# Stages 12 and 13 scaled and transposed earlier, and one second product moved ahead of the last state visit, in a fused RWKV and MLP kernel

## The chip, the cores and the metric

The kernel runs on one core of one Trainium2 chip. The metric is the device time of one execution in microseconds (us).

## The reference

A linear attention over 4 batches, 8 heads, 768 tokens and 48 channels is followed by a two-layer MLP on 3072 tokens of 384 channels:

```python
for t in range(S):
    cur = einsum('bhd,bhe->bhde', u * k[t], v[t])
    y[t] = einsum('bhd,bhde->bhe', r[t], state + cur)
    state = w * state + einsum('bhd,bhe->bhde', k[t], v[t])
x = y.transpose(0, 2, 1, 3).reshape(B * S, H * D)
h = x @ w_in                       # 384 -> 2048
out = maximum(0.01 * h, h) @ w_out # 2048 -> 384
```

## The kernel before

The tokens are cut into chunks of 128, which makes 24 stages: four batches by six chunks, the four batches side by side. Stages n and n+4 are neighbours in time of one batch, and the state goes from one to the other. Within a chunk the recurrence is a masked product of matrices. From stage 12 on an even stage is "swapped": its two halves of 64 tokens lie in exchanged order, and one load (L266) brings one half for two stages, so that stage 12 needs the loads named 12 and 14.

The order of all work is written out by hand in the string ORDER. Each word is one step, and `run` walks through the words and puts the step's instructions at the end of the queue of their engine. Every engine works through its queue in that order; semaphores are set where one engine needs another's result. PSUM banks are given out in the order of the words too. The words that matter here, for a stage n:

- `k`, `r`, `v`: the loads of the stage, issued from POOL (GpSimd).
- `Pq`, `Pk` (prep_half, L437, DVE): r and k scaled by tables of decays into qk. `X..T` (turn_dma, L442): a DMA transpose of qk into tp, issued from SP.
- `q` (row_sums, L466, L468, L470, DVE): three operations that give s_tok, the sums for the token's own term. `Q` (diag_tile, L477, POOL): two tiles with s_tok on the diagonal, written into at.
- `A` or `B` (L529, L548, PE): the products of transposed r and k, for one stage or a pair; `Ma`, `Mb` (L563, DVE) copy their lower triangle into at. B6 is the pair 12 and 13, B7 is 14 and 15, B11 is 22 and 23.
- `Y` (L719, PE): y from at, v, tp and the state; `y` (L733, ACT) copies it to xT.
- `K` (L595, PE): the stage's part of the state; `S` (L671, DVE) adds it to the state; `s` (L689, DVE) multiplies by the decay over a chunk.
- `J` (L758, PE): the MLP's first product for two stages in eight tiles, `j` (L769, ACT) their leaky ReLU into gT.
- `H` (L782, PE): the MLP's second product for one stage; `h` (L794, ACT) copies it to out_sb, and SP issues the store (L802, or L799 for swapped stages).

A round in the middle of the kernel takes two stages through each step: two Y, two K, one B, eight J and two H.

SP's queue holds both transposes and stores, in the order of the words. POOL's holds the loads and the diagonal tiles. There are six buffers each of qk, tp, at and of the state, four each of s_tok, ku, rku, sum_t and out_sb, and two of xT and gT.

Of the kernel before, what the change touches and what calls it, by code (L numbers as in the profile page):

```python
# [35 lines left out]
j2.1 P6k P7k G2.0 r7 q7 X6T J2.6 j2.6 J2.3 j2.3 k8 G3.0 J2.7 j2.7 k9 r9 j2.2 J2.5 P7q g3.0 g2.3 X7T J2.0 H1 h1 r8 q8  # L36
g2.0 Q6 P9k j2.0 P8k H0 j2.5 H3 Q7 A6 P9q X9T P8q X8T v6 A7 M6a v7 M7a g2.1 ts qtabs ktabs H2 h2 v9 v11 v10 M6b Y6 M7b
tris y6 Q8 Y7 y7 K5 r11 K6 S6 r10 k10 S5 v8 k11 k12 k14 K7 S7 q9 Q9 h0 h3 J3.0 j3.0 J3.1 j3.1 J3.2 j3.2 J3.3 j3.3 J3.4
j3.4 J3.5 j3.5 J3.6 j3.6 J3.7 j3.7 A8 A9 M8a M8b M9a M9b P10q P10k X10T P11q P11k X11T r12 r14 k13 r13 q10 Q10 q11 Q11
H4 h4 Y8 Y9 y8 y9 K8 K9 S8 S9 s8 s9 H5 h5 J4.0 j4.0 J4.1 j4.1 J4.2 j4.2 J4.3 j4.3 J4.4 j4.4 J4.5 j4.5 J4.6 j4.6 J4.7  # L40
j4.7 P12q P12k X12T P13q P13k X13T q12 q13 A10 A11 M10a M10b M11a M11b v12 v14 k15 r15 v13 v15 Q12 Q13 H6 h6 H7 h7 Y10
Y11 y10 y11 K10 K11 B6 M12a M12b M13a M13b S10 S11 P14q P14k X14T P15q P15k X15T s10 s11 q14 q15 J5.0 j5.0 J5.1 j5.1
k16 k18 r16 r18 k17 r17 Q14 Q15 J5.2 j5.2 J5.3 j5.3 J5.4 j5.4 J5.5 j5.5 J5.6 j5.6 J5.7 j5.7 H8 h8 H9 h9 Y12 Y13 y12
y13 K12 K13 B7 M14a M14b M15a M15b S12 S13 P16q P16k X16T P17q P17k X17T s12 s13 q16 q17 J6.0 j6.0 J6.1 j6.1 v16 v18
k19 r19 v17 v19 Q16 Q17 J6.2 j6.2 J6.3 j6.3 J6.4 j6.4 J6.5 j6.5 J6.6 j6.6 J6.7 j6.7 H10 h10 H11 h11 Y14 Y15 y14 y15
K14 K15 B8 M16a M16b M17a M17b S14 S15 P18q P18k X18T P19q P19k X19T s14 s15 q18 q19 J7.0 j7.0 J7.1 j7.1 k20 k22 r20
r22 k21 r21 Q18 Q19 J7.2 j7.2 J7.3 j7.3 J7.4 j7.4 J7.5 j7.5 J7.6 j7.6 J7.7 j7.7 H12 h12 H13 h13 Y16 Y17 y16 y17 K16
K17 B9 M18a M18b M19a M19b S16 S17 P20q P20k X20T P21q P21k X21T s16 s17 q20 q21 J8.0 j8.0 J8.1 j8.1 v20 v22 k23 r23
v21 v23 Q20 Q21 J8.2 j8.2 J8.3 j8.3 J8.4 j8.4 J8.5 j8.5 J8.6 j8.6 J8.7 j8.7 H14 h14 H15 h15 Y18 Y19 y18 y19 K18 K19
B10 M20a M20b M21a M21b S18 S19 P22q P22k X22T P23q P23k X23T s18 s19 q22 q23 J9.0 j9.0 J9.1 j9.1 Q22 Q23 J9.2 j9.2  # L50
J9.3 j9.3 J9.4 j9.4 J9.5 j9.5 J9.6 j9.6 J9.7 j9.7 H16 h16 Y20 Y21 y20 y21 B11 M22a M22b M23a M23b H17 h17 J10.0 j10.0
J10.1 j10.1 J10.2 j10.2 J10.3 j10.3 J10.4 j10.4 J10.5 j10.5 J10.6 j10.6 J10.7 j10.7 H18 h18 Y22 Y23 y22 y23 H19 h19
J11.0 j11.0 J11.1 j11.1 J11.2 j11.2 J11.3 j11.3 J11.4 j11.4 J11.5 j11.5 J11.6 j11.6 J11.7 j11.7 H20 h20 H21 h21 H22
h22
"""


# [855 lines left out]
```

## Time and profile before

| | us |
|---|---|
| median of 3 runs | 168.83 (167.63 to 169.45) |
| the profiled execution's own time | 167.48 |
| its span, first to last instruction | 165.6 |
| PE busy | 159.2 (96%) |
| DVE busy | 106.6 (64%) |
| ACT busy | 90.2 (54%) |
| POOL busy | 109.5 (66%) |

The granted clock of TensorE is 1.00 throughout. PE is the matmul unit, PEld its weight loads, DVE the vector engine, ACT the scalar engine, POOL GpSimd and SP the engine that only issues. Times in the profile are counted from the span's start. A row of a timeline gives start, length, engine, line, operation and tiles; in brackets stands the idle time before it and what ended that.

### The profile page before, as it was taken

The numbers are of one execution on the slowest core, as the hardware profiler recorded it, in microseconds if no ns is written. First come the engines' busy times: TensorE is split into PE (matmuls) and PEld (weight loads), VectorE is DVE, ScalarE is ACT, GpSimd is POOL, SyncE is SP. The second block draws the span as 40 slices with busy tenths as digits, with TensorE's granted clock in tenths as the row PEclk, the third lists the DMA queues.
The fourth block names the chain that finished last, engine by engine and source line by source line (L and its number), as shares of the span: only waits on it lengthen the run. The fifth ranks groups of instructions, "written<-read, shape, count | busy, mean of one in ns | idle before, by whom it ended". The sixth has DMA issues, their size and how long they took to land.

```text
span 165.6 us, 5519 instructions
## 1 busy us (share of the span) xinstructions
PE 159.2 (96%) x2397; PEld 122.3 (74%) x2397; DVE 106.6 (64%) x254; ACT 90.2 (54%) x170; POOL 109.5 (66%) x125
## 2 busy tenths in 40 slices
PE   4899999999999999999999999999999999999993
PEld 4678999986568678668668678678678668678663
DVE  7789998278777699948939939939939970000000
ACT  3855893875078339346447437438439429449121
POOL 8999798987999969999099399299370360000000
DMA  7999999999999998999969969969950621020023
GB/s 107 149 143 158 172 189 187 182 151 175 91 175 211 123 127 176 131 180 138 92 153 105 141 150 82 130 170 82 157 131 7 127 51 48 0 64 35 16 82 99
DMA packets 101366, 20.23 MB, mean 122 GB/s; under 512 B 94555, under 2 KB 101342, under 8 KB 101342
## 3 DMA queue, kind: packets, MB, share of 16 engines
q0 software_dynamic: 76512, 10.03, 92.8%
q1 hardware_dynamic: 23790, 9.65, 29.1%
q8 instruction: 19, 0.31, 0.8%
q10 hardware_dynamic: 1040, 0.20, 0.6%
q14 instruction: 5, 0.04, 0.1%
HBM read 20.45 MB, written 4.72 MB: 152 GB/s over the span
## 4 chain that ended last, share of the span: by engine, by line
PE 91%; DMA 4%; POOL 2%; ACT 1%; issue 1%; POOLq 0%; ACTq 0%
PE ps L758 39%; PE ps L782 38%; PE ps L719 6%; DMA v_sb<-in_v_dram 4%; PE ps L529 2%; PE ps L548 2%; PE ps L500 1%; PE ps L604 1%; POOL k_sb L269 1%; PE ps L595 1%; POOL r_sb L269 1%; PE ps L712 1%; ACT out_sb L794 0%; POOL w_in_sb L279 0%; ACT xT L733 0%
## 5 line engine op out<-in xcount | busy, mean ns | idle before, releaser
L758 PE MATMUL ps<-xT,w_in_sb 128*128 128x256 bf16 (+1 forms) x672 | 66.5, 259 | 0.0
L782 PE MATMUL ps<-w_out_sb,gT 128*128 128x384 bf16 (+2 forms) x400 | 64.8, 320 | 0.0
L769 ACT ACTIVATE gT<-ps 128x512 bf16<-128x512 f32 x96 | 56.3, 598 | 14.1 <-PE ps L758 10.1
L758 PEld LDWEIGHTS ps<-xT,w_in_sb 128*128 128x128 bf16 x672 | 57.7, 98 | 6.3
L477 POOL TENSOR_TENSOR at<-ident,s_tok 128x512 bf16<-128x512 bf16 x40 | 42.1, 1082 | 25.1 <-DVE s_tok L470 25.1
L782 PEld LDWEIGHTS ps<-w_out_sb,gT 128*128 128x128 bf16 x400 | 38.0, 98 | 23.0
L794 ACT ACTIVATE out_sb<-ps 128x384 f32<-128x384 f32 (+2 forms) x25 | 11.8, 478 | 46.4 <-PE ps L782 46.4
L563 DVE CAST_PREDICATED at<-mask,ps 128x512 bf16<-128x512 uint16 x28 | 17.9, 685 | 3.2 <-PE ps L529 3.0
L563 DVE CAST_PREDICATED at<-mask_s,ps 128x512 bf16<-128x512 uint16 x12 | 7.7, 687 | 14.2 <-PE ps L548 13.8
L269 POOL DMA_DIRECT2D v_sb<-in_v_dram x18 | 16.4, 927 | 0.0
L269 POOL DMA_DIRECT2D r_sb<-in_r_dram x17 | 15.7, 930 | 0.1
L269 POOL DMA_DIRECT2D k_sb<-in_k_dram x17 | 15.7, 927 | 0.0
L468 DVE TENSOR_TENSOR rku<-r_sb,ku 128x384 bf16<-128x384 bf16 x20 | 12.2, 612 | 1.4 <-DMA r_sb<-in_r_dram 0.7
L733 ACT ACTIVATE xT<-ps 128x384 bf16<-128x384 f32 x24 | 10.8, 490 | 3.1 <-PE ps L719 3.0
L470 DVE TENSOR_REDUCE s_tok<-rku 128x8 f32<-128x384 bf16 x20 | 11.1, 553 | 0.7
L719 PE MATMUL ps<-at,v_sb 128*32 128x128 bf16 x384 | 10.8, 223 | 0.0
L719 PEld LDWEIGHTS ps<-tp,st 128*32 128x32 bf16 x240 | 7.3, 96 | 3.0 <-issue 2.9
L466 DVE TENSOR_TENSOR ku<-k_sb,u_tab 128x384 bf16<-128x384 bf16 x20 | 7.9, 394 | 2.0 <-DMA k_sb<-in_k_dram 1.8
L719 PEld LDWEIGHTS ps<-at,v_sb 128*32 128x32 bf16 x384 | 8.8, 98 | 0.5 <-issue 0.2
L719 PE MATMUL ps<-tp,st 128*32 128x128 bf16 x240 | 9.1, 221 | 0.0
L671 DVE TENSOR_TENSOR sum_t<-ps,st 64x192 bf16<-64x192 f32 x24 | 8.5, 353 | 0.6
L437 DVE TENSOR_TENSOR qk<-k_sb,ktab 128x384 bf16<-128x384 bf16 x17 | 7.5, 447 | 1.0 <-DMA k_sb<-in_k_dram 1.0
(82 smaller groups left out, 124.1 us busy)
## 6 DMA issues: line engine op xcount, KB each, us to landing
out_dram<-out_sb SPq DMA_DIRECT2D x17, 192.0 KB, 3.3
v_sb<-in_v_dram POOLq DMA_DIRECT2D x24, 96.0 KB, 4.6
r_sb<-in_r_dram POOLq DMA_DIRECT2D x23, 96.0 KB, 4.9
k_sb<-in_k_dram POOLq DMA_DIRECT2D x23, 96.0 KB, 5.6
w_in_sb<-in_moe_w_in_dram POOLq DMA_DIRECT2D x4, 384.0 KB, 6.4
w_out_sb<-in_moe_w_out_dram POOLq DMA_DIRECT2D x4, 384.0 KB, 7.0
out_dram<-out_sb SPq DMA_DIRECT2D x12, 96.0 KB, 2.2
tp<-qk SPq DMA_TRANSPOSE x18, 4.4
```

The costliest lines, as they stand in the source:

```text
L269: add("pool", lambda: G.dma_start(dst, src), R=pace, W=[(which, n)], dma=f"{which}{n}")
L468: add("dve", lambda: V.tensor_tensor(rku[i2][:, :], r_of(n), ku[i2][:, :], ALU.mult), R=loaded("r", n) + [("ku", i2)], W=[("rku", i2)])
L470: add("dve", lambda: V.tensor_reduce(s_tok[i2][:, :], hd(rku[i2][:, :]), AX.X, ALU.add), R=[("rku", i2)], W=[("s", i2)])
L477: add("pool", lambda hh=hh, s_of=s_of: G.tensor_tensor(at[ia][:, hh, :, :], ident[:, :].unsqueeze(1).to_broadcast([128, NP, 128]), s_of.un ...
L563: add("dve", lambda: V.copy_predicated(at[n % NAT][:, hh, :, :], tri[:, :].bitcast(mybir.dt.uint16).unsqueeze(1).to_broadcast([128, NP, 12 ...
L671: add("dve", lambda part=part: V.tensor_tensor(both[part], kv[part[0]], st[n % NT][part], ALU.add), R=[key, ("st", n % NT)], W=[("sum", n ...
L719: last = PE.matmul(ps_y[32 * q:32 * q + 32, 128 * s:128 * s + 128], a, m, start=not whole and step == 0, stop=step == len(columns[q]) - 1)
L733: add("act", lambda: A.activation(xT[ix][:, :, 128 * slot:128 * slot + 128], ps_y[:, 0:HD].rearrange("p (s t) -> p s t", t=128), AF.Copy), ...
L758: last = PE.matmul(ps_g[:, step * f:step * f + step], w_in_sb[:, s, 128 * fb:128 * fb + 128], xT[ix][:, s, t], start=s == 0, stop=s == NSL ...
L769: add("act", lambda: A.activation(gT[ig][:, fb0:fb0 + count, t], ps_g[:, :].rearrange("p (f t) -> p f t", t=128 * width), AF.Prelu, alpha= ...
L782: last = PE.matmul(ps_o[:, 0:c1 - c0], gT[ig][:, s, 128 * slot:128 * slot + 128], w_out_sb[:, s, c0:c1], start=s == 0, stop=s == NFB - 1)
L794: add("act", lambda: A.activation(out_sb[io][:, c0:c1], ps_o[:, 0:c1 - c0], AF.Copy), R=[key], W=held)
```

## The change

Only ORDER changes. Word by word, with the line breaks of the string taken out:

```diff
 r12 r14 k13 r13 q10 Q10
-q11 Q11
+P12q P12k X12T
 H4 h4 Y8 Y9 y8 y9 K8 K9 S8 S9
+q11 Q11 P13q P13k X13T
 s8 s9 H5 h5 J4.0 j4.0
...
 J4.7 j4.7
-P12q P12k X12T P13q P13k X13T
 q12 q13 A10 A11 M10a M10b M11a M11b
...
 H16 h16
+H17 h17
 Y20 Y21 y20 y21 B11 M22a M22b M23a M23b
-H17 h17
 J10.0 j10.0
```

On DVE, the scaling of stage 12 now stands right behind the sums of stage 10, then S8 and S9, then the sums of stage 11, the scaling of 13, and s8 and s9. POOL's own order is the same as before, and so is PE's but for H17, which goes ahead of Y20 and Y21; on ACT h17 goes ahead of y20 and y21. On SP the transpose of stage 12 goes ahead of the store of stage 4, and that of stage 13 ahead of the store of stage 5. Some PSUM banks are other ones at the end: before, the eight tiles of J10 took the banks left by h16, y20, y21, the four masks of 22 and 23, and h17, in this order; now the first takes that of h16, the second that of h17, the third and fourth those of y20 and y21, and the last four those of the masks.

More of the change, by code (lines that the diff above doesn't have):

```diff
@@ L38 @@
 tris y6 Q8 Y7 y7 K5 r11 K6 S6 r10 k10 S5 v8 k11 k12 k14 K7 S7 q9 Q9 h0 h3 J3.0 j3.0 J3.1 j3.1 J3.2 j3.2 J3.3 j3.3 J3.4
[L39 to L52, printed above, removed]
@@ L53 @@
-J11.0 j11.0 J11.1 j11.1 J11.2 j11.2 J11.3 j11.3 J11.4 j11.4 J11.5 j11.5 J11.6 j11.6 J11.7 j11.7 H20 h20 H21 h21 H22
-h22
+j3.4 J3.5 j3.5 J3.6 j3.6 J3.7 j3.7 A8 A9 M8a M8b M9a M9b P10q P10k X10T P11q P11k X11T r12 r14 k13 r13 q10 Q10 P12q
+P12k X12T H4 h4 Y8 Y9 y8 y9 K8 K9 S8 S9 q11 Q11 P13q P13k X13T s8 s9 H5 h5 J4.0 j4.0 J4.1 j4.1 J4.2 j4.2 J4.3 j4.3
+J4.4 j4.4 J4.5 j4.5 J4.6 j4.6 J4.7 j4.7 q12 q13 A10 A11 M10a M10b M11a M11b v12 v14 k15 r15 v13 v15 Q12 Q13 H6 h6 H7
+h7 Y10 Y11 y10 y11 K10 K11 B6 M12a M12b M13a M13b S10 S11 P14q P14k X14T P15q P15k X15T s10 s11 q14 q15 J5.0 j5.0 J5.1
@@ new lines @@
+j5.1 k16 k18 r16 r18 k17 r17 Q14 Q15 J5.2 j5.2 J5.3 j5.3 J5.4 j5.4 J5.5 j5.5 J5.6 j5.6 J5.7 j5.7 H8 h8 H9 h9 Y12 Y13
+y12 y13 K12 K13 B7 M14a M14b M15a M15b S12 S13 P16q P16k X16T P17q P17k X17T s12 s13 q16 q17 J6.0 j6.0 J6.1 j6.1 v16
+v18 k19 r19 v17 v19 Q16 Q17 J6.2 j6.2 J6.3 j6.3 J6.4 j6.4 J6.5 j6.5 J6.6 j6.6 J6.7 j6.7 H10 h10 H11 h11 Y14 Y15 y14
+y15 K14 K15 B8 M16a M16b M17a M17b S14 S15 P18q P18k X18T P19q P19k X19T s14 s15 q18 q19 J7.0 j7.0 J7.1 j7.1 k20 k22
+r20 r22 k21 r21 Q18 Q19 J7.2 j7.2 J7.3 j7.3 J7.4 j7.4 J7.5 j7.5 J7.6 j7.6 J7.7 j7.7 H12 h12 H13 h13 Y16 Y17 y16 y17
@@ new lines @@
+K16 K17 B9 M18a M18b M19a M19b S16 S17 P20q P20k X20T P21q P21k X21T s16 s17 q20 q21 J8.0 j8.0 J8.1 j8.1 v20 v22 k23
+r23 v21 v23 Q20 Q21 J8.2 j8.2 J8.3 j8.3 J8.4 j8.4 J8.5 j8.5 J8.6 j8.6 J8.7 j8.7 H14 h14 H15 h15 Y18 Y19 y18 y19 K18
+K19 B10 M20a M20b M21a M21b S18 S19 P22q P22k X22T P23q P23k X23T s18 s19 q22 q23 J9.0 j9.0 J9.1 j9.1 Q22 Q23 J9.2
+j9.2 J9.3 j9.3 J9.4 j9.4 J9.5 j9.5 J9.6 j9.6 J9.7 j9.7 H16 h16 H17 h17 Y20 Y21 y20 y21 B11 M22a M22b M23a M23b J10.0
+j10.0 J10.1 j10.1 J10.2 j10.2 J10.3 j10.3 J10.4 j10.4 J10.5 j10.5 J10.6 j10.6 J10.7 j10.7 H18 h18 Y22 Y23 y22 y23 H19
@@ L55 @@
+h19 J11.0 j11.0 J11.1 j11.1 J11.2 j11.2 J11.3 j11.3 J11.4 j11.4 J11.5 j11.5 J11.6 j11.6 J11.7 j11.7 H20 h20 H21 h21
+H22 h22
 """
```

## The prediction

> **What bounds the kernel now.** I read the page's engine shares first, then the chain that ended last, then the timeline around each place where the chain is not on PE, and last the DMAs behind those places.
>
> ```profile
> PE 159.2 (96%) x2397; PEld 122.3 (74%) x2397; DVE 106.6 (64%) x254; ACT 90.2 (54%) x170; POOL 109.5 (66%) x125
> ```
>
> PE is busy for 159.2 of 165.6 us, so only what opens or closes a gap on PE counts. The chain, in order of time, shows the two places that the change touches (start, length, what):
>
> ```profile
> 72.89 0.89 PE ps L719 x56
> 73.78 0.25 PE ps L595 x32
> 74.04 0.21 issue
> 74.25 0.54 PE ps L548 x17
> ...
> 80.14 5.20 PE ps L782 x32
> 85.34 0.90 PE ps L719 x56
> 86.23 0.25 PE ps L595 x32
> 86.48 0.47 PE ps L548 x32
> ...
> 128.79 2.61 PE ps L782 x16
> ...
> 135.96 5.24 PE ps L758 x48
> ```
>
> A middle round is Y Y, K K, B (L719, L595, L548) and then the eight J (L758), with no gap at 86. Two rounds differ: B6 (stages 12, 13) starts 0.21 late at 74.25, and B11 (22, 23), by the timeline of PE, starts 0.43 late:
>
> ```profile
> 132.06 0.23 PE L719 MATMUL ps<-at,v_sb 128*32 128x128 bf16 x4
> 132.71 0.48 PE L548 MATMUL ps<-tp 48*64 48x128 bf16 x25 [0.43 <-ACT xT L733]
> ```
>
> The profile names ACT's xT, but B's other inputs are the transposes. The instructions of L442 in narrow windows give their issue (first and last start) and time to landing, for X13T and X23T:
>
> ```profile
> L442 SPq DMA_TRANSPOSE tp<-qk x1: 1898/1898/1898, 67.1 to 67.1; - x1
> DMA to landing us min/median/max: 7.0/7.0/7.0
> ...
> L442 SPq DMA_TRANSPOSE tp<-qk x1: 1335/1335/1335, 129.5 to 129.5; - x1
> DMA to landing us min/median/max: 3.2/3.2/3.2
> ```
>
> 67.1 + 7.0 = 74.1 and 129.5 + 3.2 = 132.7: both pairs start when their second transpose lands. ACT is the nearest event, not the cause. So the change aims at 0.21 + 0.43 us; no other PE gap is in its reach.
>
> **Part 1: P12, X12T, P13, X13T earlier.** No instruction is added. Before, DVE and POOL ran so in this stretch:
>
> ```profile
> 60.22 1.08 DVE L468 TENSOR_TENSOR rku<-r_sb,ku 128x384 bf16<-128x384 bf16 x1
> 61.34 0.55 DVE L470 TENSOR_REDUCE s_tok<-rku 128x8 f32<-128x384 bf16 x1
> 61.81 1.50 DVE L671 TENSOR_TENSOR sum_t<-ps,st 64x192 bf16<-64x192 f32 x4
> 63.34 1.80 DVE L689 TENSOR_TENSOR st<-sum_t,wl 64x192 bf16<-64x192 bf16 x4
> 66.25 0.35 DVE L466 TENSOR_TENSOR ku<-k_sb,u_tab 128x384 bf16<-128x384 bf16 x1
> 66.64 0.36 DVE L468 TENSOR_TENSOR rku<-r_sb,ku 128x384 bf16<-128x384 bf16 x1
> 69.58 2.48 DVE L563 CAST_PREDICATED at<-mask,ps 128x512 bf16<-128x512 uint16 x4
> ...
> 60.01 4.20 POOL L477 TENSOR_TENSOR at<-ident,s_tok 128x512 bf16<-128x512 bf16 x4 [1.40 <-DVE s_tok L470]
> 64.16 1.69 POOL L266 DMA_DIRECT2D v_sb<-in_v_dram  x2
> 69.35 4.09 POOL L477 TENSOR_TENSOR at<-ident,s_tok 128x512 bf16<-128x512 bf16 x4
> 73.34 1.69 POOL L266 DMA_DIRECT2D k_sb<-in_k_dram  x2
> 82.45 3.21 POOL L477 TENSOR_TENSOR at<-ident,s_tok 128x512 bf16<-128x512 bf16 x3 [4.01 <-DVE s_tok L470]
> ```
>
> The new head of the line is P12q, which needs both halves of the swapped loads r12 and r14 (L266). r14 is the later:
>
> ```profile
> L266 POOL DMA_DIRECT2D r_sb<-in_r_dram x1: 830/830/830, 56.0 to 56.0; - x1
> DMA to landing us min/median/max: 4.6/4.6/4.6
> ```
>
> So P12q cannot start before 60.6, where q11 began at 59.84 (0.38 before the row at 60.22): DVE stands 0.75 us, and behind it wait S8, S9, q11 and, through q11, Q11 on POOL. Then there is POOL's tile product: rku took 1.08 at 60.22, beside a tile, and 0.36 at 66.64, with none; it ended when the tile did. P12q would so end at 61.3, and P12k behind the second Q10 tile, one tile (4.20/4 = 1.05) later, at 62.4. If the two slip in between tiles it is 61.6; I take 62.4, for the row at 60.22 is the same pair of operations at the same place. From there: S8, S9 1.50 (one SBUF input; their pitch is the same beside tiles) to 63.9; q11 0.35 + 0.36 + 0.55 to 65.2. Q11's two tiles then run on POOL 65.2 to 67.4, where they ended at 64.2: **POOL is 3.2 us later** (2.3 by the other end), and everything in its queue with it. P13q goes at once, P13k behind the first Q11 tile: 66.4, so X13T is issued at 66.4 and not 67.1; X12T at 62.4 instead of 65.8. With loads starting only at 67.4, both should land in the 3.2 of an undisturbed transpose to 5 us, by 71.4. **B6 no longer waits: -0.21.**
>
> The Trainium skill, page "SBUF — State Buffer", section "Who interferes with whom", says that a Vector instruction with two SBUF inputs and a GpSimd one that reads SBUF lock each other out wholly. The 1.08 against 0.36 agrees; it speaks against this change, since P12, P13 and the first decay then come under tiles. Without the lock POOL's delay would be the smaller 2.3 and the sum 0.2 to 0.3 us better.
>
> What is late next on DVE: of the four parts of s8, s9 (1.80 beside a tile) the first stands behind the second Q11 tile, to about 67.6, and the other three take some 0.8: 68.4. q12 started at 66.25 and now at 68.4. q12 and q13 took 3.33 to 69.58; less the stretched rku among them (0.72) 2.6: 71.0. Four masks M10, M11 (2.48) end at 73.5, 72.1 before. Y11 needs the last; PE reaches Y11 half-way through 72.89 to 73.78, at 73.34. **Wait 0.1 us**, with ends 0 (P12 slips in) and 0.8 (the rku stays stretched).
>
> What is late next on POOL: the loads v12 to v15 from 67.4, needed for K12 at 86; Q12, Q13 at 72.6 to 76.7, just ahead of the masks M12, M13 at 75 to 77; then k16 to r17, six loads from 76.5 rather than 73.34. POOL's 4.01 us of idle time before 82.45 takes the rest up. But X14T and X15T are issued at 79.5 and 80.8, until now after that train, hereafter within it. How a transpose fares then is bounded by X15T of before and X13T (7.0, 2.95 us after the first load of a train of six at 64.16); between stands X17T, 6.35 us after the train that began at 86.60:
>
> ```profile
> 86.60 1.69 POOL L266 DMA_DIRECT2D v_sb<-in_v_dram  x2
> ...
> L442 SPq DMA_TRANSPOSE tp<-qk x1: 2514/2514/2514, 80.8 to 80.8; - x1
> DMA to landing us min/median/max: 4.4/4.4/4.4
> ...
> L442 SPq DMA_TRANSPOSE tp<-qk x1: 1814/1814/1814, 93.0 to 93.0; - x1
> DMA to landing us min/median/max: 4.0/4.0/4.0
> ```
>
> X15T will come 4.3 us after its train's first load; on the line from X13T to X17T that is 7.0 - 3.0 * 1.35/3.4 = 5.8, landing at 86.6. PE reaches B7 at 86.48 - 0.21 + 0.1 = 86.37. **Wait 0.23 us** at B7, with ends 0 (4.4) and 1.4 (7.0, landing 87.8).
>
> The Trainium skill, page "DMA: Bandwidth & Descriptors", section "Queues, rings and completion order", has each DMA engine alternate between the queues that have work. By that a transpose at most doubles its undisturbed 3.2 us, to 6.4 as an estimate, and the worst case at B7 would be 0.8; X13T's 7.0 goes beyond it, so the row's end is kept.
>
> SP: h4's output now waits behind X12T and h5's behind X13T, 2 to 4 us. Their buffers are next written four stages on, at 95: nothing.
>
> **Part 2: H17 ahead of Y20, Y21.** PE does the same work. H16 and H17 back to back take 5.20 (row at 80.14): 128.79 to 133.99; X23T landed at 132.7, so B11 waits no more. Y20, Y21 0.90 to 134.89, B11 0.47 to 135.36. But H17 had been the cover between the last Y and J10, which needs xT from y21. ACT:
>
> ```profile
> 85.89 0.88 ACT L733 ACTIVATE xT<-ps 128x384 bf16<-128x384 f32 x2
> 131.51 0.49 ACT L794 ACTIVATE out_sb<-ps 128x384 f32<-128x384 f32 x1 [2.08 <-PE ps L782]
> ```
>
> In a middle round xT is done 0.54 after the last Y (86.77 against 86.23), which K and B (0.72) cover. Here there is no K, and B11 covers 0.47: J10 starts at 134.89 + 0.54 + 0.1 (the gap from PE's end at 131.40 to ACT's start at 131.51) = 135.53. **135.96 to 135.53: -0.43**, with ends -0.6 (xT needs no wait) and -0.2 (h17's 0.49 on ACT pushes y20). The masks of 22, 23 end at 138.1 rather than 136; J10's fifth tile, the first into their banks, starts at 135.53 + 4 * 5.24/8 = 138.15 and needs only the first of them.
>
> **Sum:** -0.21 + 0.10 + 0.23 - 0.43 = -0.31 us against the profiled execution's 167.48, which is 165.6 of span and 1.9 around it. That execution is 1.35 under the median of the runs, 168.83; I move the median by the same: **168.5 us**. What a measurement of this kernel can tell from no change is about 1%, 1.7 us, so this is "within".
>
> **Rivals.**
>
> *Slower: r14 is late and DVE stands.* P12q blocks DVE from the moment r14 is late, and all else queues behind. Another load of the same size took 6.5:
>
> ```profile
> L269 POOL DMA_DIRECT2D k_sb<-in_k_dram x1: 923/923/923, 50.4 to 50.4; - x1
> DMA to landing us min/median/max: 6.5/6.5/6.5
> ```
>
> With 6.5, r14 lands at 62.5, 1.9 later; M11 ends at 75.4, Y11 waits 2.0, B6 is at 76.1 (+1.8), X15T goes out at 82.6 in the thick of loads as late as it: 7.0 gives 89.6, B7 +3.1, less 0.43: +2.7, 171.5. From 1 us late it costs over 1%. For it: nothing stands between DVE and Y11 any more. Against it: r14 had 4.6 in a quiet stretch.
>
> *The new waits do not come* (P12 slips between tiles): -0.21 - 0.43 = -0.64, 168.2.
>
> *Faster: unprofiled runs lose more to these transposes.* If the 1.35 us between profile and median lies in the same two landings, -0.64 - 1.35 = -2.0: 166.8. For it: 7.0 against 3.2 shows how much a landing varies. Against: nothing shows where the 1.35 lies.
>
> *That it doesn't do what it says:* X12T, X13T earlier by 3.4 and 0.7 only; the second part is sure, as PE's order changes. It falls into the forecast.
>
> **Numbers.** Forecast 0.39, no new waits 0.16 (both within 1%), r14 late 0.27 (slower), unprofiled waits 0.18 (faster). Range: from 167.0, which takes in half of the faster case, to 170.9, which takes in the slower one to two thirds; the likeliest's own range, from its bounds, is 168.0 to 169.9 (-0.21 - 0.6 and 87.8 - 86.48 - 0.2).
>
> **What would show it.** Right: B6 follows K13 without a gap; P12q starts near 60.6; k16's load is issued near 76.5; X15T lands after 86; L548 at about 135 has no gap before it, and J10 one of 0.2. Wrong: a PE gap before Y11 over 0.8 us, POOL late by under 2 us, X15T landing in 4.5 us, or a PE gap anywhere not named here.

## The result, and the profile after

| | before | after |
|---|---|---|
| median of 22 runs, us | 167.97 (167.15 to 170.71) | 170.25 (168.86 to 174.74) |
| ratio | | 1.0097, 95% interval 1.0070 to 1.0123 |
| the profiled execution, us | 167.48 | 169.47 |
| its span, us | 165.6 | 167.7 |

The kernel became slower by 1.0%, about 1.6 us; the forecast was 0.3 us faster. The ratio leaves out the executions more than 1.5% above the fastest of their kernel, six of after and one of before; the medians hold all of them.

The first line of the page shows that PE is busy for 0.6 us more than before; its share fell because the span grew by 2.1:

```profile
PE 159.8 (95%) x2397; PEld 122.4 (73%) x2397; DVE 107.6 (64%) x254; ACT 90.6 (54%) x170; POOL 109.7 (65%) x125
```

The chain that ended last, from stage 10's second product to B7 (start, length, what):

```profile
73.31 0.27 issue
73.58 0.60 PE ps L719 x28
74.17 0.02 issue
74.20 0.50 ACT xT L733
74.70 0.07 issue
74.77 0.57 PE ps L719 x28
75.35 0.25 PE ps L595 x31
75.59 0.47 PE ps L548 x32
76.06 5.35 PE ps L758 x48
...
87.20 0.86 ACT xT L733 x2
88.06 0.85 issue
88.91 0.54 PE ps L548 x17
```

Before, the two Y took one unbroken 0.89 from 72.89. Now there are three holes: 0.27 ahead of Y10, one between Y10 and Y11, and one ahead of B7, which starts at 88.91 and not at 86.48. B6 itself waits for nothing any more. The waits of PE have the same places, with ACT named as the nearest event:

```profile
PE ps L548 <- ACT xT L733: 1.2, 1, 1.2
PE ps L719 <- ACT xT L733: 0.6, 1, 0.6
```

What was really late ahead of the Y stands on DVE, and ahead of B7 on POOL and SP (DVE and POOL by their timelines, then the transposes of 14 and 15):

```profile
61.22 0.47 DVE L437 TENSOR_TENSOR qk<-r_sb,qtab_s 128x384 bf16<-128x384 bf16 x1 [0.87 <-DMA r_sb<-in_r_dram]
61.61 1.19 DVE L437 TENSOR_TENSOR qk<-k_sb,ktab_s 128x384 bf16<-128x384 bf16 x1
68.85 0.36 DVE L466 TENSOR_TENSOR ku<-k_sb,u_tab 128x384 bf16<-128x384 bf16 x1
70.49 1.08 DVE L468 TENSOR_TENSOR rku<-r_sb,ku 128x384 bf16<-128x384 bf16 x1
72.19 2.48 DVE L563 CAST_PREDICATED at<-mask,ps 128x512 bf16<-128x512 uint16 x4
```

```profile
65.68 2.21 POOL L477 TENSOR_TENSOR at<-ident,s_tok 128x512 bf16<-128x512 bf16 x2 [3.09 <-DVE s_tok L470]
67.83 1.70 POOL L266 DMA_DIRECT2D v_sb<-in_v_dram  x2
77.03 1.70 POOL L266 DMA_DIRECT2D k_sb<-in_k_dram  x2
81.20 0.93 POOL L269 DMA_DIRECT2D r_sb<-in_r_dram  x1
```

```profile
L442 SPq DMA_TRANSPOSE tp<-qk x2: 1241/2059/2877, 80.8 to 82.1; - x2
DMA to landing us min/median/max: 6.7/6.7/6.8
```

The masks of 10 and 11 run from 72.19 to 74.67, where they ended at 72.1. POOL stood 3.09 for q11's sums, so that the loads k16 to r17 begin at 77.03 and not at 73.34, and X14T and X15T travel beside them: 6.7 each, where X15T took 4.4.

Between the first starts of J3, B6, B7 and J11 on PE, the two traces read, in us:

| stretch | before | after | difference |
|---|---|---|---|
| start to J3 (nothing changed here) | 49.26 | 49.69 | +0.43 |
| J3 to B6 | 24.98 | 25.84 | +0.86 |
| B6 to B7 | 12.17 | 13.39 | +1.22 |
| B7 to J11 | 60.83 | 60.52 | -0.31 |
| J11 to end | 18.34 | 18.24 | -0.10 |

The first row lies ahead of everything that was changed, and reads 49.26 to 51.88 in the kernels of this document that are the same up to there. The others give +1.67, which is the 1.0% of the runs.

### The profile page after: what moved, and what is told of

Read it like the earlier page. It is cut to its first block, busy times and chain, and to the rows that moved or that the text cites. A ratio compares the mean times of both kernels' runs of the same rounds, so it can differ in the third digit from the quotient of the medians.

```text
span 167.7 us, 5519 instructions
## 1 busy us (share of the span) xinstructions
PE 159.8 (95%) x2397; PEld 122.4 (73%) x2397; DVE 107.6 (64%) x254; ACT 90.6 (54%) x170; POOL 109.7 (65%) x125
## 4 chain that ended last, share of the span: by engine, by line
PE 90%; DMA 4%; ACT 2%; POOL 1%; issue 1%; DVE 0%; POOLq 0%; ACTq 0%; DVEq 0%
PE ps L758 38%; PE ps L782 38%; PE ps L719 5%; DMA k_sb<-in_k_dram 4%; PE ps L500 2%; PE ps L529 2%; PE ps L548 1%; ACT xT L733 1%; PE ps L604 1%; ACT out_sb L794 1%; PE ps L595 1%; POOL r_sb L269 1%; PE ps L712 1%; POOL w_in_sb L279 0%; PE ps L578 0%
## 5 line engine op out<-in xcount | busy, mean ns | idle before, releaser
L794 ACT ACTIVATE out_sb<-ps 128x384 f32<-128x384 f32 (+2 forms) x25 | 11.8, 478 | 45.3 <-PE ps L782 45.3
L468 DVE TENSOR_TENSOR rku<-r_sb,ku 128x384 bf16<-128x384 bf16 x20 | 11.5, 575 | 1.9 <-DMA r_sb<-in_r_dram 1.2
L437 DVE TENSOR_TENSOR qk<-k_sb,ktab 128x384 bf16<-128x384 bf16 x17 | 8.3, 491 | 1.5 <-DMA k_sb<-in_k_dram 1.5
```

Of the source, the lines that this page charges most:

```text
L468: add("dve", lambda: V.tensor_tensor(rku[i2][:, :], r_of(n), ku[i2][:, :], ALU.mult), R=loaded("r", n) + [("ku", i2)], W=[("rku", i2)])
L794: add("act", lambda: A.activation(out_sb[io][:, c0:c1], ps_o[:, 0:c1 - c0], AF.Copy), R=[key], W=held)
```

## The experiments

Each kernel differs from one of the two by a few words of ORDER. Stretches are given in the order J3 to B6, B6 to B7, B7 to J11, J11 to end. A train is a row of loads that POOL issues one right behind the other. The last two columns count from the first load of the train that X15T travels with, k16 to r17 (73.34 in before, 77.03 in after): when X15T was issued, and when it landed. Kernel 10 stands at the end, with its own numbers.

| kernel | ratio to before (95%) | stretches, us | X15T issued | landed |
|---|---|---|---|---|
| before | 1 | 24.98, 12.17, 60.83, 18.34 | +7.45 | +11.87 |
| after | 1.0097 (1.0070 to 1.0123) | 25.84, 13.39, 60.52, 18.24 | +5.04 | +11.79 |
| 1, part 1 alone | 1.0106 (1.0055 to 1.0157) | 25.83, 13.95, 60.83, 18.34 | +5.05 | +12.36 |
| 2, part 2 alone | 1.0007 (0.9966 to 1.0048) | 24.86, 12.16, 60.52, 18.25 | +7.34 | +11.50 |
| 3, q11 kept early | 0.9958 (0.9916 to 1.0001) | 24.70, 12.16, 60.52, 18.24 | +6.93 | +11.35 |
| 4, q11 behind S9 alone | 1.0077 (1.0036 to 1.0118) | 25.85, 12.16, 60.83, 18.29 | +7.12 | +11.25 |
| 5, masks ahead of q13 | 1.0195 (1.0159 to 1.0232) | 24.70, 14.56, 62.19, 18.23 | +4.17 | +11.63 |
| 6, P12 then q11 | 1.0031 (1.0002 to 1.0061) | 24.70, 12.82, 60.52, 18.38 | +5.62 | +11.80 |
| 7, three loads hoisted | 1.0017 (0.9980 to 1.0053) | 25.83, 12.16, 60.52, 18.24 | +5.05 | +9.32, behind 3 loads |
| 8, q13 ahead of q12 | one execution, 169.26 us | 25.12, 13.68, 60.52, 18.32 | +4.34 | +11.37 |
| 9, both waits away | 0.9952 (0.9914 to 0.9990) | 24.70, 12.18, 60.52, 18.25 | +4.17 | +8.75, behind 3 loads |

**1 and 2: the parts by themselves.** After with H17 h17 back in its old place; before with H17 h17 moved.

```diff
 H16 h16
-H17 h17 Y20 Y21 y20 y21 B11 M22a M22b M23a M23b
+Y20 Y21 y20 y21 B11 M22a M22b M23a M23b H17 h17
```

> The change without its second part: H17 stays behind B11. Theory (the earlier P12 and P13 delay q11, q12, q13 on DVE and Q11 on POOL; the masks of 10, 11 come late for Y10 and Y11, and the loads k16 to r17 come to lie beside X14T and X15T): B7 about 2.0 us later than before against the rounds ahead, and nothing regained at the end: +2.0 us, 1.2%. Rival (a part of the loss sits in the new order at the end): +1.0 to +1.6.

> Before, with H17 alone moved ahead of Y20, Y21. Theory: B11 finds its transposes landed, J10 waits 0.2 us for xT instead: -0.4 us, -0.25%. Rival (the move costs, because the J10 tiles wait for banks or xT): 0 or more.

The loss is all in part 1. Part 2 gains 0.31 ahead of J11 and 0.09 behind it in the profile; the runs of kernel 2 cannot resolve 0.4 us.

**3: q11 kept early.** After with q11 Q11 directly behind Q10 again, so that POOL is not late.

```diff
-q10 Q10 P12q P12k X12T H4 h4 Y8 Y9 y8 y9 K8 K9 S8 S9 q11 Q11 P13q
+q10 Q10 q11 Q11 P12q P12k X12T H4 h4 Y8 Y9 y8 y9 K8 K9 S8 S9 P13q
```

> The whole change, but q11 and Q11 stay directly behind q10 and Q10; P12, X12T, then S8, S9, P13, X13T, s8, s9. Theory (the harm comes through the late s_tok of 11 and the stand of DVE): POOL runs as before, DVE ends q13 and the masks where it did (72 us), B6 and B7 do not wait: -0.6 us against before, -0.4%. Rival (the harm comes from X12T, X13T earlier on SP and in the DMAs, or from S8, S9 later): still +1 us or more.

Both waits are gone, and the rest of the change is worth 0.70 us in the four stretches; the interval of the runs just reaches no change. The chain from Y10 to B7 has no hole (it lies later as a whole: this execution lost 1.7 ahead of J3, at Y6, of which more below):

```profile
75.51 0.90 PE ps L719 x56
76.40 0.25 PE ps L595 x32
76.65 0.47 PE ps L548 x32
...
87.67 0.90 PE ps L719 x56
88.57 0.25 PE ps L595 x29
88.82 0.47 PE ps L548 x32
```

**4: q11 behind S9 alone.** The other side of 3: before, with nothing moved but q11 Q11.

```diff
-q10 Q10 q11 Q11 H4 h4 Y8 Y9 y8 y9 K8 K9 S8 S9 s8 s9
+q10 Q10 H4 h4 Y8 Y9 y8 y9 K8 K9 S8 S9 q11 Q11 s8 s9
```

> Before, with q11 and Q11 moved behind S8, S9 and nothing else. It delays Q11 on POOL without moving a transpose. Theory (a short delay is taken up by the 0.8 us that the masks of 10, 11 have ahead of Y11, and POOL 1.3 us later still clears X14T, X15T): Y11 does not wait, B6 waits for X13T as before, X15T lands in 4.4 to 5 us: 0 +- 0.3 us. Rival (any delay of Q11 costs): +1 us.

My expectation missed. POOL is late here too, by 1.3 us at the loads v12 to v15, and as P13 is in its old place, X13T travels with them: it landed 9.7 after the train's first load (10.0 in before: 67.1 + 7.05 - 64.16), and B6 waits 1.08. So a late POOL is by itself enough for a loss, 0.8 us of the four stretches and 0.8% (0.4 to 1.2) in the runs; it takes another place.

```profile
65.43 1.70 POOL L266 DMA_DIRECT2D v_sb<-in_v_dram  x2
...
74.42 0.78 issue
75.20 0.54 PE ps L548 x17
...
L442 SPq DMA_TRANSPOSE tp<-qk x2: 1248/1495/1742, 66.5 to 67.8; - x2
DMA to landing us min/median/max: 5.7/6.5/7.3
```

**5: masks ahead of q13.** After with the masks of 10 and 11 no longer behind q13's sums on DVE.

```diff
-q12 q13 A10 A11 M10a M10b M11a M11b
+q12 A10 A11 M10a M10b M11a M11b q13
```

> The whole change, with the masks of 10, 11 ahead of q13 on DVE. Theory (two separate waits): Y10 and Y11 no longer wait, B6 comes 0.2 us earlier than before; but POOL's loads are as late as in the change, X15T takes 6 to 7 us and B7 waits 0.5 to 1.5: +0.3 to +1.0 us against before. Rival (the wait at B7 follows from the one at Y11): B7 does not wait, -0.5 us.

The waits at Y10 and Y11 are gone (24.70), but the kernel is slower than after, and the loss of 1.95% is far above what was expected. X15T goes out still nearer to the train's start and takes 7.46. B7 starts 39.26 behind J3, where it was 39.23 in after: PE only comes there 1.14 earlier and waits that much longer, 2.3. Then the eight J behind it take 7.01 instead of 5.35. The table of windows (PE, PEld, DVE, ACT, POOL busy, then the granted clock, DMA's share and GB/s) shows why, and the chain above it the place:

```profile
82.32 7.46 DMA tp<-qk
89.78 0.09 issue
89.87 0.54 PE ps L548 x17
90.41 7.01 PE ps L758 x48
```

```profile
88.00:90.00 2.00, 0.13 (x12) 0.16 (x16) 0.00 (x0) 0.00 (x0) 2.00 (x4) 1.00 1.74 243
90.00:92.00 2.00, 2.00 (x42) 1.53 (x38) 1.46 (x3) 0.48 (x1) 2.00 (x3) 0.68 1.78 116
92.00:94.00 2.00, 2.00 (x11) 1.44 (x10) 1.94 (x5) 0.72 (x2) 1.35 (x2) 0.50 2.31 129
94.00:96.00 2.00, 2.00 (x20) 1.75 (x18) 1.92 (x8) 1.70 (x3) 0.00 (x0) 0.97 1.74 91
```

**6 and 8: two more orders.** In 6 P12 X12T stays ahead of q11, but Q11 goes ahead of S8 and S9. In 8 q13 goes ahead of q12.

```diff
-P12q P12k X12T H4 h4 Y8 Y9 y8 y9 K8 K9 S8 S9 q11 Q11 P13q
+P12q P12k X12T q11 Q11 H4 h4 Y8 Y9 y8 y9 K8 K9 S8 S9 P13q
```

```diff
-q12 q13 A10 A11
+q13 q12 A10 A11
```

> The whole change, with q11 and Q11 behind P12, X12T but ahead of S8, S9: the wait for r14 stays, Q11 is 1.7 us late instead of 3.2. Theory (what costs is the sum of delays beyond 0.8 us on DVE and about 2 on POOL): M11 ends about 1.1 us later than before, Y11 waits 0 to 0.4, X15T takes 4.5 to 5 us, B7 waits not at all: -0.4 to 0 us. Rival (the wait for r14 is what costs): +1 us or more.

> The whole change with q13 ahead of q12 on DVE; the time should be that of the change. In every run so far the product rku of stage 13 took 1.08 us instead of 0.36 though no tile ran on POOL. If that belongs to the place (the second of two sums), it will now be rku of stage 12; if it belongs to stage 13's data, the first of the two will be long; if a load's issue on POOL does it, either or none.

Kernel 6 gives half the delay: no wait at the Y, 0.59 at B7. The expectation missed B7: X15T took 6.17, not 4.5 to 5, and the kernel is 0.3% slower than before. In 8 neither rku is stretched, and J3 to B6 shrinks from 25.84 to 25.12, by the 0.72 that a stretched rku costs; 0.29 of it comes back as a longer wait at B7:

```profile
70.62 0.36 DVE L468 TENSOR_TENSOR rku<-r_sb,ku 128x384 bf16<-128x384 bf16 x1
...
71.59 2.48 DVE L563 CAST_PREDICATED at<-mask,ps 128x512 bf16<-128x512 uint16 x4
```

**7: three loads hoisted.** After with k16, k18 and r16 issued in the 3 us in which POOL stands idle.

```diff
-S8 S9 q11 Q11 P13q
+S8 S9 k16 k18 r16 q11 Q11 P13q
...
-J5.1 j5.1 k16 k18 r16 r18 k17 r17 Q14 Q15
+J5.1 j5.1 r18 k17 r17 Q14 Q15
```

> The whole change, with the loads k16, k18, r16 issued in the 3.1 us in which POOL stands before Q11, so that only r18, k17, r17 are left behind Q13. Theory (X15T is slow because six loads lie beside it): X15T lands in 4.4 to 5 us, B7 waits at most 0.3 more than B6 made it late, +0.5 to +0.7 us against before instead of +1.7. Rival (X15T is late only because it is issued late, or slow whatever lies beside it): B7 as in the change, +1.7.

The train beside X14T and X15T is three loads shorter. X15T lands 9.3 after its first load and not 11.8, and B6 to B7 is back at 12.16 while the waits at Y10 and Y11 stay (25.83). So the wait at B7 is there because of the loads beside X15T, and not because of the wait at the Y. The other way round, taking away the wait at the Y alone gains nothing, as kernel 5 shows, because B7 is held by the landing.

**9: both edits, 5 and 7 together.**

> The changed kernel with both edits that took one wait each: the loads k16, k18, r16 ahead of Q11, and the masks of 10 and 11 ahead of q13. Theory (the two waits are separate and are the whole loss): Y10, Y11 and B7 follow without a gap, J3 to B6 takes 24.70, B6 to B7 12.2, B7 to J11 60.52 with the granted clock at 1.00 throughout; against before -0.28 for B6 and -0.31 for H17, -0.6 us in all, ratio 0.996 to 0.998. Rival (q13 behind the masks makes Q13 so late that r18, k17, r17 now lie beside X14T and X15T): B7 waits 0.5 to 1.5 us, ratio 1.000 to 1.006.

The three stretches that the expectation names came out as it says, and this kernel beats both, by 0.5% against before: 167.86 us (166.96 to 169.78) beside 168.72 of the runs of before on the same chip. The chain from K10 to B7, where B7 now follows the K of its round as B6 does:

```profile
74.21 0.25 PE ps L595 x32
74.46 0.47 PE ps L548 x32
...
85.49 0.90 PE ps L719 x56
86.39 0.25 PE ps L595 x32
86.64 0.47 PE ps L548 x32
```

**10: q11 early and the masks of 6, 7 first.** Kernel 3 lost 1.71 at Y6, because M6 and M7 stand on DVE behind P8q, which stands behind a late load of r. Here, in kernel 3, P9q X9T P8q X8T go behind M7b.

```diff
-A6 P9q X9T P8q X8T v6 A7 M6a v7 M7a g2.1 ts qtabs ktabs H2 h2 v9 v11 v10 M6b Y6 M7b tris
+A6 v6 A7 M6a v7 M7a g2.1 ts qtabs ktabs H2 h2 v9 v11 v10 M6b Y6 M7b P9q X9T P8q X8T tris
```

> The changed kernel with q11 Q11 back behind Q10, and further P9q X9T P8q X8T behind M7b, so that the masks of 6 and 7 don't stand behind P8q on DVE. Theory (the wait ahead of Y6 of 0 to 1.7 us in the profiles so far comes from P8q behind the late load r8, and has nothing to do with the change): no gap ahead of Y6, the rest as with q11 kept early, ratio 0.992 to 0.996. Rival (X9T and X8T, issued 3 us later, land after 54.6): A8 or A9 waits 0.5 to 2 us, ratio 0.999 to 1.008.

The gap ahead of Y6 is gone, and the rival's came, larger than it said: the transposes now went out among loads, took 7.2 and 7.6, and A8 waited 4.0. The kernel is 3.2% slower (1.0322, 1.0268 to 1.0375). Again the clock fell behind the wait, and the H that followed took 4.39 in place of 2.71:

```profile
52.25 7.19 DMA tp<-qk
...
59.57 0.62 PE ps L529 x16
60.19 4.39 PE ps L782 x16
```

```profile
60.00:62.00 2.00, 2.00 (x16) 1.02 (x10) 1.92 (x4) 0.00 (x0) 0.00 (x0) 0.66 2.62 143
62.00:64.00 2.00, 2.00 (x8) 0.95 (x7) 1.97 (x7) 0.00 (x0) 0.00 (x0) 0.50 1.80 101
```

## Why the prediction was wrong

The mechanisms were the right ones, and nearly in the right places; two sizes were off, and both in the same direction. Against the 24.70 that kernels 3 and 9 take without a wait, and the 12.17 of before, the four terms were:

| term | forecast | bounds given | measured |
|---|---|---|---|
| B6 waits no more | -0.21 | | -0.28 |
| Y10, Y11 wait for the masks | +0.10 | 0 to 0.8 | +1.14 |
| B7 waits for X15T | +0.23 | 0 to 1.4 | +1.22 |
| H17 ahead of Y20, Y21 | -0.43 | -0.6 to -0.2 | -0.41 |
| sum | -0.31 | | +1.67 |

- **B6 and H17: right.** X13T was issued at 67.0 ahead of the loads and B6 has no gap. J10 starts behind xT from y21. The 0.41 is after against before in the last two stretches, and so is kernel 1 against after; kernel 2 against before gives 0.40.
- **DVE's order down to q12: right.** r14 landed 4.8 after its issue, DVE stood 0.87 (0.75 forecast), P12k ended at 62.8 (62.4 forecast, and the trace lies 0.43 later from its start on), q12 began at 68.85 (68.4 forecast). The rival that r14 comes late was not the cause.
- **The step that failed on DVE** is "less the stretched rku among them (0.72)". I held that the 1.08 of q13's rku came from a tile on POOL, and that it would go with the tile; the prediction gives no row for that. It stayed, with no tile beside it: POOL issued loads from 67.83 until 73.07. It had been so in before, where the tiles ended at 64.21 and the next began at 69.35 (DVE and POOL by their timelines):

```profile
67.88 1.08 DVE L468 TENSOR_TENSOR rku<-r_sb,ku 128x384 bf16<-128x384 bf16 x1
...
67.59 1.79 POOL L269 DMA_DIRECT2D v_sb<-in_v_dram  x2
```

That is 0.72 of the miss in this term. Most of the rest is that PE stops twice: each time the Y behind the hole starts anew, 0.60 + 0.57 for the two where one unbroken run takes 0.89. The first of these stops, 0.27 ahead of Y10, is one that the prediction doesn't name. I gave 0.8 as the outer end, named for the stretch, and took the value near the other; the 1.14 lies beyond even that end. Kernel 8 removes the stretch and gets 0.72 back; 5 and 9 remove the whole term.
- **The step that failed at B7** is the price of 5.8 for X15T, on a line from X13T to X17T by the time since the train's first load. X15T was issued 5.0 us after that load, where the line would say 5.2, and took 6.75. Its issue came 0.84 later than forecast, and PE came to B7 about 0.96 later (both less the 0.43), so that the price, 0.95 too small, is the miss. For this transpose the landing held in the runs better than the duration: in nine kernels with six loads in this train, X15T landed 11.3 to 12.4 us after the train's first load, whether it had been issued 4.2 or 7.5 us after it; in kernel 10, issued 8.6 after it, it landed 12.85 after. Behind three loads (7 and 9) it was 8.8 to 9.3. A row of before had this number: 80.8 + 4.4 - 73.34 = 11.9. With it, and the train at 76.5 as forecast, X15T lands at 88.4 and not at 86.6; the trace has 88.8, with its 0.43. But that this was the row to take is known from the runs alone: X13T's row gives 10.0 and X17T's 93.0 + 4.0 - 86.6 = 10.4, by which X15T would land at 86.5 to 86.9, about as forecast. Why this train is slower to land than those stays open.
- **POOL's lateness, 3.2 us: right** (77.03 less 73.34 less the 0.43 is 3.26). I used it for single loads and transposes, and did not see that it is what the whole change hangs on. Kernel 3 shows that: with q11 and Q11 early, and so POOL and the masks on time, the rest of the change is 0.4% faster (0.9916 to 1.0001), and of the 0.70 us in its stretches 0.29 are ahead of B7, from the early P12 and P13.
- **The rule of the Trainium skill on the DMA queues** ("DMA: Bandwidth & Descriptors", "Queues, rings and completion order"), by which a transpose at most doubles its 3.2 us to 6.4 as an estimate, doesn't bound it here: 6.7 to 7.8 beside six loads, in after and kernel 1. Keeping the row's end was right.

What stays open is why q13's rku takes 1.08. It does so behind q12 in before, after and kernels 1 to 4, 6, 7 and 10 alike, and takes 0.36 when q13 stands ahead of q12 or behind the masks. Beside tiles the stretch agrees with the Trainium skill's "SBUF — State Buffer", "Who interferes with whom" (P12k's 1.19 ended 0.2 behind the tile); without a tile no run here explains it. So the 1.08 at 60.22, on which the prediction rests the tile's part, is weak evidence by itself, as q13's was the same without one. Nor does a tile always stretch: in 5 and 9 a tile began 0.03 and 0.01 behind the start of q13's rku and ran beside the rest of it, and the rku took 0.36.

## What to carry to other kernels

Ahead of a move on one engine, follow each result that it delays into the queue of the engine that needs it: here 3 us of POOL's idle time looked free, but its queue also issues the loads, and what counted was which transposes their trains then met. A transfer that joins a train of others has no price of its own: with six loads beside it X15T took 4.1 to 7.5 us, and its landing, counted from the train's first load, stayed within 1.1 us in nine of ten kernels. Take that landing from the same train, as X17T, X19T and X21T landed about 1 us earlier in theirs. Taking away one wait gains nothing while the next thing in line is held by something else, as in kernel 5. And where a long duration is to be subtracted, show that its cause is the one that goes away.

## What the runs showed of the hardware

- A wait of PE of 2.3 us and more cost more than itself. After gaps of 2.30 (kernel 5) and 3.96 (kernel 10) the granted clock went to 0.50 for 3.4 us, worked out from the windows of kernel 5 as (0.32 + 0.50 + 0.03) * 2 / 0.5, and the next products took 1.66 and 1.68 longer (5.35 of after, 2.71 of kernel 9 for the same H); after the gaps of 1.71 (3) and 1.72 (1) it stayed at 1.00. The mean granted clock over the whole execution is 0.99 in five of the six executions of kernel 5, and 0.98 or 0.99 in all six of kernel 10. The Trainium skill, "TensorE: Matmul & The Clock Gate", "HAM oscillation — how this bites in real kernels", gives "no PE-idle gaps >~3.4µs", about 1.67 us of throttled time each time, and half of the throttled time as the loss. That half agrees, 1.66 of 3.4; the throttled time is twice the page's here, and in kernel 5 a gap of 2.30 was enough.
- A DMA transpose issued with no load under way took 3.1 to 3.2 (X13T of after, issued at 67.0 ahead of its train, and X23T of before). Between 4.2 and 7.5 us after the first load of its train, an earlier issue gained X15T nothing: it landed 11.3 to 12.4 after that load. Earlier in a train of six it did gain: X13T, issued 0.6 to 3.0 after the first load (before, kernels 2 to 4, 6 and 10), landed 5.5 after it when issued 0.6 behind it, and 10.0 when issued 3.0 behind it. X17T, X19T and X21T, issued 5.9 to 6.5 after, landed at 10.1 to 11.4.
